# A recurrent-memory attention kernel that plans its own issue order by longest path, with attention for eight heads of both layers at once

## The chip, the cores and the metric

The kernel runs on one core of one Trainium2 chip. Its time is the device time in microseconds (us) of one execution. A time is the median of the runs quoted. The core has a matrix engine (PE, with weight loads shown apart as PEld), a vector engine (DVE), a scalar engine (ACT), a general engine (POOL) and a DMA-issuing engine (SP). The profile also gives the granted clock of the matrix engine: 1.0 is full speed, 0.5 half speed.

## The reference, cut to what matters

```python
def _A_ref(x, mem0, Wq, Wk, Wv, Wo, seg_len):          # 32 heads of 128; x is 2048 x 512
    mem = mem0                                          # 8 rows
    for s in range(n_seg):                              # 64 segments of 32 rows
        h = jnp.concatenate([mem, x[:, s*seg_len:(s+1)*seg_len, :]], axis=1)   # 40 rows
        q, k, v = (einsum('btd,dhe->bhte', h, W) for W in (Wq, Wk, Wv))
        p = _softmax(jnp.where(mask, q @ k.T * scale, -1e9))
        o = einsum('bhte,hed->btd', p @ v, Wo)
        mem = o[:, :M, :]                               # the memory goes into the next segment
        outs.append(o[:, M:, :])
...
x = x + _A_ref(_layernorm(x), A_mem0, A_Wq, A_Wk, A_Wv, A_Wo, A_seg_len)      # layer 1
x = x + _B_ref(_layernorm(x), B_w1, B_w2)                                     # dense 512 -> 1376 -> 512
x = x + _A_ref(_layernorm(x), A_mem0, A_Wq, A_Wk, A_Wv, A_Wo, A_seg_len)      # layer 2, same weights
x = x + _B_ref(_layernorm(x), B_w1, B_w2)
```

Eight rows of each segment's output are the memory of the next, so the 64 segments of a layer are a chain. Both kernels let layer 2 run six segments behind layer 1 and put the two layers' segments side by side: 70 steps, 58 of them with both layers, 12 with one. After every fourth segment of a layer, a group of 128 rows goes through a dense layer and a layernorm.

## The kernel before

The program is written step by step, and the framework's scheduler sets the order on each engine. The recurrent chain has a high priority; what is left fills the gaps.

```python
def layernorm_T(x_g):                 # statistics on DVE and POOL, then a transpose on PE
    ...
    nc.vector.tensor_scalar(out=xn[:], in0=x_g[:], scalar1=mv[:, 0:1], scalar2=rstd[:, 0:1], ...)
    tp = ps_fill.tile([128, NC4, 128], BF, tag="fill")
    for c4 in range(NC4):
        nc.tensor.transpose(tp[:, c4, :], xn[:, c4 * 128:(c4 + 1) * 128], ident[:])
    ...
for k in range(nsteps):
    place_x_values(k); load_group(...); prep_x(k + 1)     # x values: matmuls on 64-column tiles
    with tc.high_priority(offset=PRIO):
        for hf in range(2):                               # 16 heads each
            for (h0, nh) in ((16 * hf, 6), (16 * hf + 6, 6), (16 * hf + 12, 4)):
                qk_batch(HT, h0, nh, a_lo, a_hi)          # 24 (or 16) query, then as many key matmuls: full tiles
            for a in act:
                sps[(a, hf)] = s_matmuls(a, hf)           # mask (full tile) and scores (64-column tiles)
            if hf == 0:
                mem_values(k)                             # 2 x 16 matmuls on 32-column tiles
        for hf in range(2):
            for a in act:                                 # softmax of 16 heads of one layer
                ...                                       # max, subtract: DVE; exp: ACT; sum, reciprocal: DVE
                nc.gpsimd.tensor_tensor(out=P[:, :, b, 0:L], ...)   # product: POOL
        ...                                               # transposes, attention times V (row tiles)
        wo = ...                                          # next memory: 32 matmuls on 32-column tiles
    wx = ...                                              # projection of x rows: 64 matmuls on 32-column tiles
    ...                                                   # residual adds; dense layer when a group is full
```

A "32-column tile" uses a quarter of the array's columns, and four such matmuls for different quarters follow each other; a "row tile" uses part of its rows. In what follows, a change of tile shape is a place in PE's order where a matmul of one class (full tile, 64 columns, 32 columns, row tile) follows one of another. I counted them in the built kernels' order: 2233 in this one.

## Time and profile before

| | before |
|---|---|
| time, median of 3 runs | 2715.88 us (2715.72 to 2721.2) |
| span of the profiled run, granted clock | 2708.6 us, 0.907 |
| PE busy; sum of gaps between its matmuls (idle) | 2278.6 us; 426 us |
| layernorm transposes waiting for DVE | 256.4 us in 63 waits |
| changes of tile shape | 2233 |

From the page of the kernel before: the span, the busy time of each engine, the busy share of PE in 40 slices in tenths, the granted clock in the same slices, and the shares of the chain of work that ended last.

```profile
span 2708.6 us, 89958 instructions
PE 2278.6 (84%) x40852; PEld 1442.6 (53%) x40852; DVE 1271.6 (47%) x2873; ACT 655.5 (24%) x1420; POOL 332.1 (12%) x863
PE   2989878887987978888887987888788797888898
PEclk9999889898898979989898998989888897989999
PE 67%; DVE 18%; POOL 5%; DMA 4%; issue 4%; ACT 1%; SPq 0%; POOLq 0%; ACTq 0%; DVEq 0%
```

PE is the main engine, but most slices stand at 8, and the clock stands at 8 or 7 (below 90%) in 18 of the 40. The waits view names the engine and the line that wait, then whom they wait for, the total us, the times and the longest:

```profile
PE tp L178 <- DVE xn L174: 256.4, 63, 5.1
PE tp L368 <- POOL P_172 L360: 29.2, 64, 1.0
PE tp L368 <- POOL P_166 L360: 21.7, 64, 0.9
```

The layernorm's transposes stand in PE's order about 4 us too early, 63 times, and PE executes in that order. The timeline shows this, and other things (start and length in us, engine and line, output <- inputs, tile, shapes, count, and in brackets the idle time before and what ended it; the length includes the last matmul's modelled end, so rates are read from start to start).

```profile
83.48 0.76 PE L302 MATMUL qp<-HT_156,Wk_sb 128*128 128x40 bf16 x24
84.08 0.75 PE L302 MATMUL qp<-HT_156,Wq_sb 128*128 128x40 bf16 x24
...
88.45 0.77 PE L302 MATMUL qp<-HT_156,Wq_sb 128*128 128x40 bf16 x24
89.19 1.05 PE L282 MATMUL vm<-Wv_sb,HT_156 128*32 128x512 bf16 x16
90.17 0.77 PE L302 MATMUL qp<-HT_156,Wk_sb 128*128 128x40 bf16 x24
...
1308.43 0.61 PE L178 MATMUL tp<-ident,xn 128*128 128x128 bf16 x4 [3.19 <-DVE xn L174]
1313.97 0.61 PE L178 MATMUL tp<-ident,xn 128*128 128x128 bf16 x4 [4.92 <-DVE xn L174]
...
1330.92 3.17 PE L397 MATMUL wo<-Wo_sb,OT 128*32 128x512 bf16 x27
...
1406.10 1.69 PE L397 MATMUL wo<-Wo_sb,OT 128*32 128x512 bf16 x27
```

First: 24 query/key matmuls take 0.60 us where the same shape follows (83.48 to 84.08), and 0.74 us where a 32-column matmul follows (88.45 to 89.19); the change costs 0.14 us there. The 16 memory-value matmuls take 0.98 us before a change, though at 54 ns each they stream for 0.87. Second: the two waits of the layernorm transposes. Third: 27 matmuls of the memory projection take 3.17 us in one step and 1.69 in another. That is the half clock, as the windows view shows around the slow ones (window, its us, PE busy and matmuls, granted clock, DMA share, GB/s):

```profile
1316.00:1318.00 2.00, 2.00 (x12) 0.50 0.00 0
1318.00:1320.00 2.00, 2.00 (x18) 0.83 0.00 0
1320.00:1322.00 2.00, 2.00 (x38) 1.00 0.00 0
...
1326.00:1328.00 2.00, 0.89 (x14) 1.00 0.00 0
1328.00:1330.00 2.00, 2.00 (x39) 0.73 0.00 0
1330.00:1332.00 2.00, 2.00 (x24) 0.50 0.00 0
```

### The profile page before, as it was taken

The page shows a single profiled execution, that of the slowest core. Times are in us where ns is not written, and L with a number is a line of the kernel's source. Part 1 is how long each engine was busy: PE and PEld are TensorE (multiplying, and loading weights), DVE is VectorE, ACT ScalarE, POOL GpSimd, SP SyncE. Part 2 cuts the span into 40 slices and gives each one's busy share as a digit, 9 for nine tenths or more (in the row PEclk, how much of TensorE's full clock was granted, in tenths as well). Part 3 has the DMA queues.
Part 4 walks back from the last instruction along what each step waited for, and adds up shares of the span by engine and source line. Part 5 has one row for each costly group of instructions (what it writes and reads, how often), then busy time and mean ns, then how long its engine had stood idle before and what let it go on. Part 6 is the DMA issues. An engine that isn't in the chain of part 4 may idle for free.

```text
span 2708.6 us, 89958 instructions
## 1 busy us (share of the span) xinstructions
PE 2278.6 (84%) x40852; PEld 1442.6 (53%) x40852; DVE 1271.6 (47%) x2873; ACT 655.5 (24%) x1420; POOL 332.1 (12%) x863
## 2 busy tenths in 40 slices
PE   2989878887987978888887987888788797888898
PEld 1555545555554645555554554555455464555555
DVE  1444445454444445544444454544454444555443
ACT  0222222222222222222222222222222222222222
POOL 2011111011101101101111111111110110111000
PEclk9999889898898979989898998989888897989999
DMA  8000001010001001001001000101100110100000
GB/s 295 16 15 18 21 21 24 13 23 15 21 22 23 18 19 23 16 19 24 15 22 23 16 22 21 24 14 23 23 14 22 23 24 14 23 14 22 18 18 14
DMA packets 39245, 71.52 MB, mean 26 GB/s; under 512 B 13168, under 2 KB 20336, under 8 KB 38864
## 3 DMA queue, kind: packets, MB, share of 16 engines
q1 hardware_dynamic: 33296, 52.34, 8.3%
q8 instruction: 320, 5.24, 0.8%
q10 hardware_dynamic: 3824, 6.78, 0.7%
q0 software_dynamic: 1744, 6.65, 0.7%
q14 instruction: 61, 0.50, 0.1%
HBM read 21.70 MB, written 2.10 MB: 9 GB/s over the span
## 4 chain that ended last, share of the span: by engine, by line
PE 67%; DVE 18%; POOL 5%; DMA 4%; issue 4%; ACT 1%; SPq 0%; POOLq 0%; ACTq 0%; DVEq 0%
PE qp L302 24%; PE vx L257 9%; PE wo L397 7%; PE vm L282 6%; DVE x_g L424 6%; PE wx L417 6%; PE sp L315 3%; PE hp L193 2%; POOL P_172 L360 2%; DVE sm L356 2%; PE sp L311 2%; DVE stats L167 2%; PE tp L178 1%; DVE OT L390 1%; DVE es L352 1%
## 5 line engine op out<-in xcount | busy, mean ns | idle before, releaser
L307 DVE CAST KT<-qp 128x480 bf16<-128x480 f32 (+3 forms) x420 | 237.0, 564 | 416.1 <-PE qp L302 416.0
L302 PEld LDWEIGHTS <-Wq_sb 128*128 128x128 bf16 x8960 | 336.0, 99 | 71.7 <-issue 63.7
L302 PEld LDWEIGHTS <-Wk_sb 128*128 128x128 bf16 x8960 | 344.9, 99 | 25.8 <-issue 23.8
L305 ACT CAST QT<-qp 128x480 bf16<-128x480 f32 (+3 forms) x420 | 203.0, 483 | 400.8 <-PE qp L302 400.7
L417 PE MATMUL wx<-Wo_sb,OT 128*32 128x512 bf16 x4480 | 289.4, 381 | 0.6 <-ACT OT L388 0.6
L424 DVE TENSOR_TENSOR x_g<-x_g,wx 32x512 f32<-32x512 f32 x256 | 175.1, 684 | 186.2 <-PE wx L417 180.8
L397 PE MATMUL wo<-Wo_sb,OT 128*32 128x512 bf16 x2208 | 240.0, 519 | 19.6 <-ACT OT L388 16.0
L178 PE MATMUL tp<-ident,xn 128*128 128x128 bf16 x256 | 40.4, 298 | 256.4 <-DVE xn L174 256.4
L360 POOL TENSOR_TENSOR P_164<-es,sm 128x160 bf16<-128x160 f32 x128 | 55.2, 452 | 1306.1 <-DVE sm L357 1302.1
L257 PE MATMUL vx<-Wv_sb,XS_154 128*64 128x512 bf16 x1120 | 194.9, 406 | 19.2 <-DVE x_g L424 18.1
L302 PE MATMUL qp<-HT_152,Wq_sb 128*128 128x80 bf16 (+1 forms) x4480 | 193.4, 199 | 0.0
L302 PE MATMUL qp<-HT_156,Wq_sb 128*128 128x80 bf16 (+1 forms) x4480 | 192.3, 198 | 0.6 <-DVE HT_156 L409 0.6
L302 PE MATMUL qp<-HT_152,Wk_sb 128*128 128x80 bf16 (+1 forms) x4480 | 186.8, 198 | 3.2 <-DVE KT L307 1.9
L263 DVE CAST vst<-vx 128x512 bf16<-128x512 f32 x140 | 96.5, 689 | 194.9 <-PE vx L257 191.2
L302 PE MATMUL qp<-HT_156,Wk_sb 128*128 128x80 bf16 (+1 forms) x4480 | 186.6, 198 | 1.2
L417 PEld LDWEIGHTS <-OT 128*32 128x32 bf16 x4480 | 110.1, 96 | 128.0 <-issue 28.2
L178 PEld LDWEIGHTS <-xn 128*128 128x128 bf16 x256 | 21.3, 125 | 278.9 <-DVE xn L174 272.5
L257 PE MATMUL vx<-Wv_sb,XS_158 128*64 128x512 bf16 x1120 | 167.3, 448 | 1.7 <-ACT xnT L180 0.7
L350 DVE TENSOR_REDUCE mx<-sp 128x8 f32<-128x320 f32 x256 | 114.8, 487 | 45.4 <-PE sp L315 45.1
L282 PE MATMUL vm<-Wv_sb,HT_152 128*32 128x512 bf16 x1120 | 90.0, 389 | 49.3 <-DVE HT_152 L321 36.4
L354 ACT ACTIVATE es<-es 128x320 f32<-128x320 f32 x256 | 109.7, 468 | 85.4 <-DVE es L352 85.0
L397 PEld LDWEIGHTS <-OT 128*32 128x32 bf16 x2208 | 70.2, 118 | 112.1 <-issue 61.3
(1114 smaller groups left out, 2820.7 us busy)
## 6 DMA issues: line engine op xcount, KB each, us to landing
Vs_162<-vst SPq DMA_DIRECT2D x128, 128.0 KB
Vs_168<-vst SPq DMA_DIRECT2D x128, 128.0 KB
Vs_162<-vms SPq DMA_DIRECT2D x256, 16.0 KB
Vs_168<-vms SPq DMA_DIRECT2D x256, 16.0 KB
Wk_sb<-in_A_Wk_dram ACTq DMA_DIRECT2D x2, 1024.0 KB
Wv_sb<-in_A_Wv_dram POOLq DMA_DIRECT2D x2, 1024.0 KB, 19.1
Wq_sb<-in_A_Wq_dram SPq DMA_DIRECT2D x2, 1024.0 KB
Wo_sb<-in_A_Wo_dram SPq DMA_DIRECT2D x2, 1024.0 KB
```

Source lines behind the costliest of these rows:

```text
L257: nc.tensor.matmul(vx[64 * b:64 * b + 64, :], lhsT=XS[:, c4, :], rhs=Wv_sb[:, c4, n * 512:(n + 1) * 512], start=(c4 == 0), stop=(c4 == NC4 ...
L263: nc.vector.tensor_copy(out=vst[:, p, :], in_=vx[:])
L282: nc.tensor.matmul(vm[32 * q:32 * q + 32, :], lhsT=HT[:, c4, SEG:SEG + 32], rhs=Wv_sb[:, c4, n * 512:(n + 1) * 512], start=(c4 == 0), stop ...
L302: nc.tensor.matmul(qp[:, hi, 0:ncol], lhsT=W_sb[:, c4, h * Dh:(h + 1) * Dh], rhs=HT[:, c4, a_lo * L:a_hi * L], start=(c4 == 0), stop=(c4 = ...
L305: nc.scalar.copy(out=dstT[:, h0:h0 + nh, a_lo * L:a_hi * L], in_=qp[:, 0:nh, 0:ncol])
L307: nc.vector.tensor_copy(out=dstT[:, h0:h0 + nh, a_lo * L:a_hi * L], in_=qp[:, 0:nh, 0:ncol])
L350: nc.vector.tensor_reduce(out=mx[:], in_=sp[:], axis=AX.X, op=ALU.max)
L354: nc.scalar.activation(out=es[:], in_=es[:], func=ACTF.Exp, scale=SCALE)
L360: nc.gpsimd.tensor_tensor(out=P[:, :, b, 0:L], in0=es[:, 4 * b:4 * b + 4, :], in1=sm[:, 4 * b:4 * b + 4].unsqueeze(2).to_broadcast([128, 4 ...
L397: nc.tensor.matmul(wo[32 * q:32 * q + 32, :], lhsT=OT[:, h, SEG:SEG + 32], rhs=Wo_sb[:, h, :], start=(t == 0), stop=(t == H // 4 - 1), til ...
L417: nc.tensor.matmul(wx[32 * q:32 * q + 32, :], lhsT=OT[:, h, XO[a]:XO[a] + SEG], rhs=Wo_sb[:, h, :], start=(t == 0), stop=(t == H // 2 - 1) ...
L424: nc.vector.tensor_tensor(out=rows, in0=rows, in1=wx[r:r + 32, :], op=ALU.add)
```

## The change

Its intent: make attention cheaper per instruction (the softmax of eight heads of both layers at once, query and key banks of four heads emptied by one copy) and remove PE's waits by a plan. The kernel no longer issues as it is written. Every piece of work becomes an operation with an engine, an estimated cost and the data that it reads and writes. A list scheduler then picks, again and again, the engine that can start earliest, and among the operations that can start within 0.05 us of that the one with the longest path of costs and latencies to the end of the program. The kernel emits in that order, and the framework's scheduler is switched off.

```diff
+PE, ACT, DVE, POOL, SP = range(5)
+LAT = (0.26, 0.16, 0.16, 0.20, 1.70)
+LOOK = 0.05
+def t_dve(n, rate=1):
+    return 0.085 + 1.042e-3 * n / rate
...
+    def order(self):
+        for o in reversed(self.ops):
+            o.rank = o.cost + LAT[o.eng] + max((s.rank for s in o.succs), default=0.0)
...
+            lo, e = best                      # earliest start of all, and its engine
+            o = max((c for c in cand[e] if c.start <= lo + LOOK), key=lambda c: (c.rank, -c.seq))
...
-            for hf in range(2):
-                for (h0, nh) in ((16 * hf, 6), (16 * hf + 6, 6), (16 * hf + 12, 4)):
-                    qk_batch(HT, h0, nh, a_lo, a_hi)
+        for p in range(4):                    # eight heads
+            for hg in (2 * p, 2 * p + 1):     # four heads: two operations of 8 matmuls for each of q and k
+                queries_keys(k, hg, a_lo, a_hi)
+            scores(k, p, a_lo, a_hi)          # both layers: one max, subtract, exp, sum, transpose and copy
...
+            for c4 in range(NC4):             # memory values: operations of 4 matmuls
+                def mm(vm=vm, pp=pp, c4=c4): ...
+                plan.op(PE, 0.216, mm, r=[("HTm", i), ("HTx", i, 1), ...], w=[vm])
...
+        for t in range(H // 2):               # x projection: operations of 4 matmuls; x values: of 2
+                plan.op(PE, 0.216, mm, r=[("OT", t // 4), ...], w=[wx])
...
+    with tc.manual_schedule():
+        for o in plan.order():
+            o.fn()
```

The matrix work is the same: 40876 matmuls instead of 40852, the 24 more being mask matmuls. In the new order I counted 4658 changes of tile shape.

## The prediction

> **What bounds the kernel now.** PE is 67% of the chain of waits, DVE 18%; PE is busy 2278.6 of 2708.6 us, not all of it useful. From start-to-start times in the timeline at granted clock 1.0, one matmul costs 35.9 ns (query/key, 80 columns; 25 ns with 40), 54 ns (memory values, both output projections: 32-column tiles), 108 ns (x values: 64-column tiles), 216 ns (second dense product), about 56 ns (first dense product, transposes), 19 to 23 ns (scores, attention). Times the counts: 1780 us. Around each change of tile shape (128, 64, 32 columns, row tiles) about 0.115 us is lost: 16 memory-value matmuls before a query matmul take 0.98 us instead of 0.87, 4 x-value matmuls 0.55 instead of 0.43. The Trainium skill ("TensorEngine Tiling (Array Packing)", Key Properties) says that changing the tiling mode drains the TensorE; the trace agrees. In the issue order I count 2233 changes: 257 us. The mean granted clock of 0.907 means about 250 us lost to half speed: after a 5 us wait, 27 memory-projection matmuls take 3.17 us instead of 1.69. The rest, about 420 us, is idle PE: 256 us in 63 waits of the layernorm transposes for DVE (about 4 us each), 50 at the start, 51 for POOL's softmax product. 1780 + 257 + 250 + 420 = 2707, the span. A full step takes 40.1 us.
>
> **What the change does.** Arithmetic and matmul counts stay (24 more mask matmuls). Query/key evictions become 16 of four heads per step instead of 12; K goes partly to ACT. Estimates from durations: DVE about 80 us less, ACT 130 more; both stay far from full. In the new order, memory values, x values, projections and dense work are cut into pieces of 2 or 4 matmuls, put between query/key groups and into the softmax and layernorm waits.
>
> - Removed: nearly all layernorm waits, most POOL waits, and with them the half clock: idle 420 to about 100 us (55 start, the rest end and steps), clock loss 250 to about 20.
> - Added: the plan's costs know nothing of tile-shape changes. I count 4658, 2425 more: +279 us, all on PE, so on the critical path. A full step has 26.5 us of streaming and about 68 changes (7.8 us): 34.3 us. Steps with one layer active may get slower (about 27 us against 23).
> - Interleaved query and key halves leave about 0.7 us to empty a bank; the pieces between just cover it (eviction 0.43 to 0.49 us plus latencies).
>
> **Prediction.** 1783 + 536 (changes) + 20 (clock) + 100 (idle) = 2440 us, 0.90 of before. Range 2310 to 2580. Faster by over 2%: 0.92; within 2%: 0.05; slower: 0.03.
>
> **What would show it.** PE busy about 95% in all slices, granted clock at least 0.98, the layernorm transposes' wait for DVE under 40 us; in the chain PE at least 85%, DVE under 8%; in the timeline, 4-matmul memory-value pieces between query matmuls at about 0.45 us with both changes (0.22 of it streaming); full steps of 34 to 35 us.
>
> **What would make it wrong.** The cost of a change: 0.08 us would give 2280, 0.15 us 2600; I measured it mostly with long runs on both sides, and short pieces may differ. Waits that the plan doesn't foresee: its DVE and ACT costs are some 15% below the trace's (320 columns on DVE 0.42 planned, 0.49 measured), and the query/key banks or the last-projection chain could leave PE idle 1 to 2 us per step (+70 to 140 us). A clock that drops although PE is nearly always busy.

## The result

| | before | after |
|---|---|---|
| time, median of 4 runs | 2717.56 us (2715.72 to 2721.2) | 2488.48 us (2479.97 to 2492.84) |
| span of the profiled run, granted clock | 2708.6 us, 0.907 | 2478.0 us, 0.979 |
| idle PE | 426 us | 173 us |
| lost to the clock, (1 - clock) x span | 252 us | 52 us |
| of it while PE was busy | 192 us | 48 us |
| changes of tile shape | 2233 | 4658 |

The ratio is 0.9152 (95% interval 0.9122 to 0.9181). The prediction of 2440 us was 48 us too low, and its range holds the result. While PE waits, half clock takes nothing from it; the row "of it while PE was busy" (half of PE's busy time under the trace's records of half clock) leaves that part out.

The lines of the page of the kernel after that answer to those of before:

```profile
span 2478.0 us, 91607 instructions
PE 2300.9 (93%) x40876; PEld 1338.7 (54%) x40876; DVE 1202.9 (49%) x2947; ACT 748.5 (30%) x1818; POOL 343.9 (14%) x910
PE   0899999999999999999999999999999999999998
PEclk9899999998999999999999999999999999999999
```

Its largest waits of PE:

```profile
PE fill_183 L326 <- DVE bf_76 L321: 60.1, 1, 60.1
PE misc_181 L614 <- POOL P_148 L605: 17.4, 6, 2.9
PE fill_184 L326 <- DVE bf_76 L321: 14.9, 10, 3.9
```

The 256 us of layernorm waits are gone but for one at the start (60.1 us) and about 17 us besides. PE stands at 9 in all slices but the first two and the last. Yet PE's busy time has grown, from 2278.6 to 2300.9 us, though the clock is better. The timeline shows why:

```profile
1302.75 0.45 PE L535 MATMUL qk_178<-HT_136,Wq_sb 128*128 128x80 bf16 x8
1303.04 0.45 PE L535 MATMUL qk_177<-HT_136,Wq_sb 128*128 128x80 bf16 x8
1303.42 0.41 PE L469 MATMUL fill_183<-Wv_sb,XS_138 128*64 128x512 bf16 x2
1303.76 0.40 PE L697 MATMUL fill_184<-Wo_sb,OT 128*32 128x512 bf16 x4
1303.98 0.39 PE L503 MATMUL st_182<-Wv_sb,HT_136 128*32 128x512 bf16 x4
1304.30 0.46 PE L535 MATMUL qk_178<-HT_136,Wk_sb 128*128 128x80 bf16 x8
```

Eight query matmuls take 0.29 us before eight of the same shape (1302.75 to 1303.04), and 0.38 before a 64-column matmul. Four 32-column matmuls take 0.22 us before others of that shape (1303.76 to 1303.98), and 0.32 before full tiles. Each change costs some 0.1 us, and nothing in the plan's costs knows of it.

### The profile page after: what moved, and what is told of

Read it like the earlier page. It is cut to its first block, busy times and chain, and to the rows that moved or that the text cites. A ratio compares the mean times of both kernels' runs of the same rounds, so it can differ in the third digit from the quotient of the medians.

```text
span 2478.0 us, 91607 instructions
## 1 busy us (share of the span) xinstructions
PE 2300.9 (93%) x40876; PEld 1338.7 (54%) x40876; DVE 1202.9 (49%) x2947; ACT 748.5 (30%) x1818; POOL 343.9 (14%) x910
## 5 line engine op out<-in xcount | busy, mean ns | idle before, releaser
L535 PEld LDWEIGHTS <-Wq_sb 128*128 128x128 bf16 x8960 | 352.1, 99 | 90.5 <-issue 86.6
L697 PE MATMUL fill_184<-Wo_sb,OT 128*32 128x512 bf16 x2560 | 252.5, 389 | 2.6 <-DVE xg_74 L707 1.7
L659 PE MATMUL st_182<-Wo_sb,OT 128*32 128x512 bf16 x2208 | 225.0, 406 | 3.1 <-ACT OT L442 2.2
L442 ACT CAST QT<-qk_177 128x320 bf16<-128x320 f32 (+1 forms) x279 | 112.5, 403 | 380.1 <-PE qk_177 L535 375.4
L442 ACT CAST QT<-qk_178 128x320 bf16<-128x320 f32 (+1 forms) x281 | 113.5, 404 | 354.3 <-PE qk_178 L535 353.9
L444 DVE CAST KT<-qk_177 128x320 bf16<-128x320 f32 (+1 forms) x218 | 100.3, 460 | 240.9 <-PE qk_177 L535 226.9
L444 DVE CAST KT<-qk_178 128x320 bf16<-128x320 f32 (+1 forms) x202 | 92.7, 459 | 190.3 <-PE qk_178 L535 174.2
L697 PEld LDWEIGHTS <-OT 128*32 128x32 bf16 x4480 | 112.1, 94 | 134.7 <-issue 84.9
L605 POOL TENSOR_TENSOR P_145<-es_162,sm_166 128x160 bf16<-128x160 f32 (+1 forms) x140 | 58.1, 435 | 861.3 <-ACT QT L442 397.8
L697 PE MATMUL fill_183<-Wo_sb,OT 128*32 128x512 bf16 x1920 | 170.2, 385 | 0.0
L469 PE MATMUL fill_183<-Wv_sb,XS_139 128*64 128x512 bf16 x664 | 143.5, 428 | 1.9 <-ACT hT_176 L360 1.9
L535 PE MATMUL qk_177<-HT_136,Wk_sb 128*128 128x80 bf16 (+1 forms) x2256 | 124.7, 199 | 5.0 <-POOL HT_136 L460 4.9
L535 PE MATMUL qk_178<-HT_136,Wk_sb 128*128 128x80 bf16 (+1 forms) x2224 | 122.3, 199 | 4.1 <-POOL HT_136 L460 3.9
L469 PE MATMUL fill_183<-Wv_sb,XS_138 128*64 128x512 bf16 x632 | 125.3, 399 | 0.7
L535 PE MATMUL qk_178<-HT_136,Wq_sb 128*128 128x80 bf16 (+1 forms) x2256 | 125.1, 200 | 0.3 <-DVE KT L444 0.3
L535 PE MATMUL qk_177<-HT_137,Wk_sb 128*128 128x80 bf16 (+1 forms) x2240 | 123.0, 199 | 0.0
L535 PE MATMUL qk_177<-HT_136,Wq_sb 128*128 128x80 bf16 (+1 forms) x2224 | 122.8, 199 | 0.1
L535 PE MATMUL qk_178<-HT_137,Wk_sb 128*128 128x80 bf16 (+1 forms) x2240 | 122.9, 199 | 0.0
L535 PE MATMUL qk_177<-HT_137,Wq_sb 128*128 128x80 bf16 (+1 forms) x2240 | 122.9, 199 | 0.0
L535 PE MATMUL qk_178<-HT_137,Wq_sb 128*128 128x80 bf16 (+1 forms) x2240 | 122.8, 199 | 0.0
L469 PEld LDWEIGHTS <-XS_139 128*64 128x64 bf16 x1120 | 62.9, 112 | 105.4 <-issue 94.5
```

The source lines that it names most:

```text
L442: nc.scalar.copy(out=out_, in_=in_)
L444: nc.vector.tensor_copy(out=out_, in_=in_)
L469: nc.tensor.matmul(vx[64 * b:64 * b + 64, :], lhsT=XS[:, c4, :], rhs=Wv_sb[:, c4, n * 512:(n + 1) * 512], start=(c4 == 0), stop=(c4 == NC4 ...
L535: nc.tensor.matmul(qp[:, hi * 2 * L:hi * 2 * L + n], lhsT=W_sb[:, c4, h * Dh:(h + 1) * Dh], rhs=HT[:, c4, c0:c1], start=(c4 == 0), stop=(c ...
L605: nc.gpsimd.tensor_tensor(out=P[:, a_lo:a_hi, :, b, 0:L], in0=es[:, a_lo:a_hi, b, :, :], in1=s.unsqueeze(3).to_broadcast([128, na, 2, L]), ...
L659: nc.tensor.matmul(wo[32 * q:32 * q + 32, :], lhsT=OT[:, h, SEG:SEG + 32], rhs=Wo_sb[:, h, :], start=(t == 0), stop=(t == H // 4 - 1), til ...
```

## The experiments

My theory had three parts. (1) The gain is idle PE and half clock removed, by the plan. (2) A good part of it is given back by 2425 more changes of tile shape, at about 0.1 us each. (3) The rival explanations are: the grouping of attention by eight heads and the smaller operations do it, whatever the order; or any list scheduling does it, and longest path is no part of it; and for the given-back part, that interleaving costs by waits and not by the changes. All kernels below gave correct results and were timed in 3 rounds. The first four (stay_p16, stay_p4, stay_m16, fifo) ran on one chip (before there: 2714.06 us, median of 7), the other four on another (before: 2708.54 us, median of 7). For the measurement of the kernel after no chip is on record (before there: 2717.56 us).

### A preference for the tile shape that PE has: three doses

The plan's choice gets a bonus for a PE operation whose first matmul has the tile shape that PE's last one had. The bonus is in us of path. Operations, costs and everything else stay. With 16 the plan stays with a shape where it can, with 4 it does so where ranks are close, and with -16 it seeks changes.

```diff
+STAY = 16            # 4 in stay_p4, -16 in stay_m16
...
-            o = max((c for c in cand[e] if c.start <= lo + LOOK), key=lambda c: (c.rank, -c.seq))
+            o = max((c for c in cand[e] if c.start <= lo + LOOK),
+                    key=lambda c: (c.rank + STAY * (e == PE and c.shape[0] == last), -c.seq))
...
+            if e == PE:
+                last = o.shape[1]
...
-                plan.op(PE, 0.216, mm, r=[("XS", i, 0), ("XS", i, 1), ("W", "v", p)],
+                plan.op(PE, 0.216, mm, shape=(64, 64), r=[("XS", i, 0), ("XS", i, 1), ("W", "v", p)],
... (shape of first and last matmul: 32-column pieces (32, 32), scores (128, 64), attention (0, 0), all else (128, 128))
```

Expected of the bonus of 16:

> One key in the planner is changed: among the PE operations that could start now, one of the tile shape that PE has just used gets 16 us added to its rank. Same operations, same costs, same buffers; tile-shape changes in the issue order fall from 4658 to 2388. If a change costs PE about 0.11 us and PE sets the time: 2488 - 2270 x 0.11 = about 2240 us (2200 to 2300). If what is left after the change is waits for other engines and shape changes are hidden or free: about 2490 us, or slower, as the longest path is no longer followed strictly.

Expected of the bonus of 4:

> The same with 4 us added: 3541 changes of tile shape. Shape-change theory: 2488 - 1117 x 0.11 = about 2365 us, up to 40 us more from waits because this plan itself has some more idle PE: 2350 to 2410. Rival (changes are free): about 2490 us or more.

Expected of the bonus of -16:

> The same with 16 us taken away, so that the planner seeks changes: 5957. Shape-change theory: 2488 + 1299 x 0.11 = about 2630 us, perhaps 60 us less since this plan has less idle PE: 2560 to 2640. Rival (changes are free): about 2490 us or less.

Measured:

| kernel | changes | time (range), us | ratio to before | idle PE, us | clock |
|---|---|---|---|---|---|
| stay_p16 | 2388 | 2151.48 (2150.27 to 2152.91) | 0.7934 | 138.1 | 0.997 |
| stay_p4 | 3541 | 2410.52 (2406.27 to 2413.5) | 0.8886 | 205.3 | 0.967 |
| after | 4658 | 2488.48 (2479.97 to 2492.84) | 0.9152 | 173.0 | 0.979 |
| stay_m16 | 5957 | 2535.29 (2531.58 to 2536.88) | 0.9345 | 128.7 | 0.993 |

The page of stay_p16:

```profile
PE 2006.1 (93%) x40798; PEld 1296.1 (60%) x40876; DVE 1195.1 (56%) x2947; ACT 752.1 (35%) x1818; POOL 349.5 (16%) x910
```

Its timeline, with whole runs of one shape where the kernel after has pieces:

```profile
1300.76 1.32 PE L540 MATMUL qk<-HT,Wq_sb 128*128 128x80 bf16 x32
1302.01 0.40 PE L664 MATMUL st<-Wo_sb,OT 128*32 128x512 bf16 x4
1302.34 1.92 PE L474 MATMUL fill<-Wv_sb,XS 128*64 128x512 bf16 x16
```

The page of stay_m16, with the same operations:

```profile
PE 2402.1 (95%) x40795; PEld 1398.9 (55%) x40876; DVE 1206.5 (48%) x2947; ACT 775.9 (31%) x1818; POOL 345.9 (14%) x910
```

And its timeline, where pieces of 4 and 8 matmuls take 0.33 and 0.39 us with a change after each. The last two lines show a change of operation without a change of tile shape:

```profile
1300.88 0.40 PE L508 MATMUL st<-Wv_sb,HT 128*32 128x512 bf16 x4
1301.21 0.46 PE L540 MATMUL qk<-HT,Wq_sb 128*128 128x80 bf16 x8
1301.60 0.40 PE L508 MATMUL st<-Wv_sb,HT 128*32 128x512 bf16 x4
...
1316.01 0.46 PE L540 MATMUL qk<-HT,Wq_sb 128*128 128x80 bf16 x8
1316.31 0.30 PE L564 MATMUL misc<-maskb,ident 128*128 128x320 bf16 x1
```

The time follows the number of changes. The cleanest pair is stay_p16 and stay_m16: same operations, idle PE 138 and 129 us (both traces lack some 80 matmul records, so both are a little too high), clock 0.997 and 0.993, and 3569 more changes take 2535.29 - 2151.48 = 383.8 us, which is 0.1075 us for one. Waits cannot be the reason, as the slower kernel waits less. Nor is it that a piece ends and another operation begins: eight query matmuls take 0.30 us before the mask, which has the same tile shape (1316.01 to 1316.31), and 0.39 us before a 32-column piece. Over the whole trace of stay_m16, the median from a query matmul's start to the next matmul's (full clock, no wait) is 36 ns before another operation of the same shape (88 cases) and 132 ns before another shape (1388 cases). Part 2 of the theory stands, and with it what the change gives back: at 0.1075 us, 2425 more changes cost 261 us; the sum of all runs below gives 226.

The direction was as expected, two of the three times were not: stay_p16 came 49 us below its range and stay_m16 25 us below its; stay_p4 lies at the upper edge of its range. The expectations counted changes alone or nearly so; stay_p16 also has 35 us less idle PE and some 40 us less loss by the clock than the kernel after, and stay_m16 44 and some 34.

"PE busy" can't tell these kernels apart: the fast one is busy for 93% of its span, the slow one for 95%. The Trainium skill ("Perfetto Trace Analysis", Identifying the Most-Contended Engine) warns that matmul busy time is no good measure of how close a kernel is to its limit; here it rises while the kernel gets slower.

The row of the kernel after is from another measurement than the doses, and one dose is not clean: stay_p4 has fewer changes than the kernel after, but 32 us more idle PE and a lower clock (0.967). A new wait of 2.68 us for a layernorm recurs every eight steps in it. Part of what it saves in changes is lost there.

### Program order in place of longest path, without and with the preference

The scheduler and the operations stay; the rank of the longest path is replaced by the place in the program.

```diff
-            o = max((c for c in cand[e] if c.start <= lo + LOOK), key=lambda c: (c.rank, -c.seq))
+            o = max((c for c in cand[e] if c.start <= lo + LOOK), key=lambda c: -c.seq)        # fifo
+            o = max((...), key=lambda c: (STAY * (e == PE and c.shape[0] == last), -c.seq))    # fifo_stay, STAY = 1
```

Expected without the preference:

> Priority by program order in place of the longest path; everything else of the planner stays. 3494 tile-shape changes, 1164 fewer, worth -128 us. If the longest path is what removes PE's idle time, layernorm and softmax waits come back by 150 to 300 us: 2500 to 2650 us. If any greedy planning in time does it, only the fewer changes count: about 2360 us.

Expected with it:

> Program order as priority, and the same tile shape first: 3114 tile-shape changes, 726 more than stay_p16 and 380 fewer than fifo. If only changes count: 2431 - 380 x 0.10 = about 2390 us and 2151 + 73 = about 2225 us cannot both hold; what lies between them is idle PE. I expect 2300 to 2400 us with idle PE near fifo's 230 us, which would show that the longest path is worth 90 us or more of idle PE.

Measured: fifo took 2430.83 us (2425.26 to 2447.01), ratio 0.8972 (0.8935 to 0.9008), with 3494 changes, idle PE 229.5 us and clock 0.978 (the profiled run is the slowest of its four; the others had 0.982 to 0.989). My expectation was a miss: plain program order is not slower than longest path, it is faster than the kernel after by some 50 us (ratios to before 0.8972 and 0.9152, from different measurements). fifo_stay took 2399.43 us (2399.22 to 2405.53), ratio 0.886, with 3114 changes, idle PE 229.9 us and clock 0.979, as expected, at the upper edge of the range. The largest waits of PE in fifo_stay, after that at the start, recur once in nearly every step:

```profile
PE st L664 <- ACT OT L447: 54.3, 68, 0.9
PE misc L639 <- DVE PT L624: 29.8, 67, 0.5
```

So longest path does do something: the idle PE is 173 us with it and 230 without, and with the preference 138 against 230. That is 57 to 92 us. But with nothing against changes, it takes 1164 more of them (4658 against 3494), and at about 0.1 us each these cost more than the waits that it removes. Longest path is worth its trouble only with the preference: 2151 against 2399 us (ratios 0.7934 and 0.886, on two chips), of which 92 us are idle PE, 726 fewer changes give some 70 to 80, and the clock (loss of 6 against 50 us) some 44; about 40 us of the difference are in none of these terms.

### The half clock by itself

In the kernel before, useless matmuls are put in front of each layernorm's transposes, into the bank that these will overwrite. This takes none of the real work away, and the real work waits as before; it only keeps PE busy in the gap.

```diff
-        tp = ps_fill.tile([128, NC4, 128], BF, tag="fill")
+        tpf = ps_fill.tile([128, 512], F32, tag="fill")
+        for _ in range(12):
+            nc.tensor.matmul(tpf[:], lhsT=ident[:], rhs=Wq_sb[:, 0, 0:512], start=True, stop=True)
+        tp = tpf[:].bitcast(BF)
```

> The kernel before, with twelve useless 128x512 matmuls before each layernorm's transposes, into the bank that the transposes overwrite: 64 x 12 x 0.216 = 166 us of extra work at full clock. The issue order puts them exactly into the layernorm waits and moves nothing else. If the rests of PE cost about 250 us through the clock: granted clock from 0.907 to 0.95 or more, and the kernel gets faster although it does more, 2500 to 2640 us. If the idle time alone cost: no faster than before, 2715 to 2880 us.

Measured: 2659.24 us (2653.8 to 2662.75), ratio 0.9811 (0.9788 to 0.9834), clock 0.951. The transposes' wait fell from 256.4 to 80.6 us:

```profile
PE tpf L182 <- DVE xn L175: 80.6, 59, 2.3
```

This kernel does 768 more matmuls, which take 166 us even at full clock, and it is faster by 1.9%: clear of zero, but at the line of 2% the verdict is "unclear". It came out above the expected range (2500 to 2640 us), and the traces show why the clock was worth less than I thought. By the mean clock, the loss went from 252 to 130 us. But of 506 us at half clock in the kernel before, PE was idle for 122; counted while PE was busy, the loss went from 192 to 130 us. With 178 us less idle PE, 166 us more work and 122 more changes (2355, about 12 us), these 62 us make some 60 us; the spans differ by 49. So the half clock is a cost of its own. What remains of it is in its windows, at the same place of a step as in the kernel before:

```profile
1298.00:1300.00 2.00, 0.89 (x15) 1.00 0.00 0
1300.00:1302.00 2.00, 2.00 (x38) 0.68 0.00 0
1302.00:1304.00 2.00, 2.00 (x28) 0.50 0.00 0
```

In this stretch PE's single gaps were 0.52 us (before the memory projection, for an eviction by ACT) and 0.60 us (before x values, for DVE), and no more than the 0.89 of 2 us were busy. The clock fell to half all the same. The Trainium skill ("TensorE: Matmul & The Clock Gate", Part 1) has the clock halved after an idle window of about 3.4 us. The waits of 3.19 and 4.92 us before 1314 agree roughly: the clock fell at 1308.4, at the end of the shorter one, when PE had been busy for 0.07 of the last 3.41 us. The same page (A second HAM failure mode) says that PE can also idle in small gaps often enough for the clock to swing between half and full; this trace agrees, with two gaps of 0.5 and 0.6 us in two us. It does not always happen: at 1402 to 1404 in the kernel before, PE was also busy for 0.89 of 2 us, and the clock stayed at 1.00. In that kernel the clock changes on a grid of 3.41 us; PE was busy for 0.67 of the grid's interval before the fall at 1328.9, and for 0.68 of that before 1404.0, where none came. So the busy share of that interval does not decide it, and what does is open.

### The new operations under the framework's scheduler

The operations of the kernel after are emitted in program order, with the priorities of the kernel before, and the framework's scheduler orders them. Buffers are taken in turn. One ring of four buffers replaces the three rings for transposed groups.

```diff
-    with tc.manual_schedule():
-        for o in plan.order():
-            o.fn()
+    for o in plan.order():                  # now the program's order
+        if o.high:                          # the recurrent chain, as before
+            with tc.high_priority(offset=10_000_000):
+                o.fn()
+        else:
+            o.fn()
```

> The changed kernel's operations (8 heads of both layers per softmax, four-head evictions), but emitted in program order and ordered by the framework's scheduler with the same priorities as the kernel before; its own planner is out. One shared ring of four for the transposed activations, as before. Tile-shape changes in the issue order: 7848, single matmuls between single matmuls. If the planned order is what gained: slower than before, 2750 to 3050 us. If the new grouping of the attention gained: about 2490 us.

Measured: 3396.87 us (3376.76 to 3422.35), ratio 1.254 (1.2469 to 1.2611), with 7848 changes, idle PE 353.4 us and clock 0.93. Slower, as the theory said, but by more than expected. The timeline shows single memory-value matmuls between single query and key matmuls, and further on four together:

```profile
1310.36 0.39 PE L476 MATMUL st<-Wv_sb,HT 128*32 128x512 bf16 x1
1310.68 0.21 PE L508 MATMUL qk<-HT,Wq_sb 128*128 128x80 bf16 x1
...
1311.35 0.40 PE L476 MATMUL st<-Wv_sb,HT 128*32 128x512 bf16 x4
1311.68 0.21 PE L508 MATMUL qk<-HT,Wq_sb 128*128 128x80 bf16 x1
```

So the regrouping alone brought no gain that shows, and the rival that "the grouping does it, whatever the order" is refuted for this scheduler. What the grouping is worth in an order of its own with as few changes as the kernel before is not separated: this run has 5615 more changes than before. Why it is so slow can be read from its trace. The one 32-column matmul at 1310.36 takes 0.32 us up to the next, and the four at 1311.35 take 0.33: a lone one costs as much as four, so a group of four that is broken pays twice. The framework's scheduler moves single matmuls, and here 1209 of 1649 runs of 32-column matmuls are no whole groups of four (nor are 188 of 380 runs of 64-column ones whole pairs). Counted at 0.216 us for each group begun, the empty quarters and halves cost about 199 us, an estimate. The kernel before has the same fault: 398 of 584 runs, about 60 us. The planned kernels have none, as their operations of 4 and 2 matmuls stay whole. So by this count part of the plan's gain is that it keeps these groups together, which I had not thought of; no run isolates it.

### The start, and the fastest version

At the start of the kernel after, PE waits 60 us. The timeline of DVE shows what for:

```profile
58.93 0.43 DVE L405 CAST xg_73<-bf_76 128x512 f32<-128x512 bf16 x1 [23.25 <-DMA bf_76<-in_A_x_dram]
...
59.47 0.55 DVE L321 TENSOR_SCALAR bf_76<-xg_72,ln_170 128x512 bf16<-128x512 f32 x1
```

The plan believes that the second group of rows is loaded in about 2 us, and puts its conversion ahead of the first group's normalisation in DVE's order. But its load stands behind the weights in its queue. The last experiment adds to stay_p16 that this data is there only after 48 us:

```diff
             x, xb = p_x.buf(), p_b.buf()
+            plan.available(xb, 48.0)
```

> stay_p16 with the loads of x after the first marked as not available to the plan before 48 us, so that the first layernorm no longer waits in DVE's queue behind a copy of x group 1, whose load stands behind the weights in the queue. PE's first wait of 60 us should become about 36 us (the memory's load lands there); by then not all weights are there: 2125 to 2145 us against 2151.

Measured: 2125.16 us (2124.81 to 2126.25), ratio 0.7843 (0.7825 to 0.7861), 26 us less than stay_p16 (the two ran on different chips; their ratios to before there are 0.7843 and 0.7934), with idle PE 106.9 us. The first wait of PE in its timeline:

```profile
36.90 0.61 PE L331 MATMUL fill<-ident,bf 128*128 128x128 bf16 x4 [36.90 <-DVE bf L326]
```

It is the fastest version, 22% below the kernel before and some 14% below the kernel after (0.7843 against 0.9152 of before). In the kernel before, PE's first matmul ran at 36.42 us, so 24 us of the start were the plan's doing, through one wrong belief.

### All runs in one sum

For each kernel, the span less idle PE, less the loss by the clock while PE is busy, less the broken groups, less 1783 us of streaming (an estimate: counts times the rates read at full clock; 1949 us in warm), divided by the number of changes:

| kernel | span, us | idle | clock loss, PE busy | broken groups | changes | rest for one change, us |
|---|---|---|---|---|---|---|
| before | 2708.6 | 426 | 192 | 60 | 2233 | 0.111 |
| warm | 2659.4 | 248 | 130 | 63 | 2355 | 0.115 |
| after | 2478.0 | 173 | 48 | 0 | 4658 | 0.102 |
| stay_p16 | 2148.6 | 138 | 6 | 0 | 2388 | 0.093 |
| stay_p4 | 2404.5 | 205 | 71 | 0 | 3541 | 0.098 |
| stay_m16 | 2535.2 | 129 | 15 | 0 | 5957 | 0.102 |
| fifo | 2444.8 | 230 | 52 | 0 | 3494 | 0.109 |
| fifo_stay | 2397.3 | 230 | 47 | 0 | 3114 | 0.108 |
| stay_x | 2123.3 | 107 | 4 | 0 | 2392 | 0.096 |
| own_sched | 3375.1 | 353 | 184 | 199 | 7848 | 0.109 |

All ten kernels, from 2123 to 3375 us, are told by the same four terms, with 0.093 to 0.115 us for a change. The rests are good to some hundredths of a us only: the streaming is an estimate, and the score matmuls, taken at 19 to 23 ns, follow each other at 13 to 14 ns in these traces (means at full clock), so that it may be some tens of us too high.

## Why the prediction was right, and where its terms were off

- **The time, 2440 us, range 2310 to 2580.** Measured 2488.48. The way to it held: 1783 us of streaming, fewer waits, less half clock, more changes.
- **"Idle 420 to about 100 us."** It went from 426 to 173. This is the term that was mis-sized most (+73 us). The start took 60 us and not 55, and about 45 us are stalls that recur every eight steps: 2.9 and 2.3 us for POOL's softmax product, 1.0 for a layernorm, 1.0 for POOL's copy of x rows into HT, the input of the queries and keys. That the wait for POOL comes from the plan's order on DVE was only argued.
- **"Clock loss 250 to about 20."** 48 us on busy PE (52 by the mean clock); the clock was 0.979 and not "at least 0.98". The 250 us of the kernel before were too many: 192 of them fell on busy PE (the rest on waits that were counted already).
- **"4658, 2425 more: +279 us."** The count was exact; a change cost 0.102 us by the sum and 0.1075 between the two clean doses, not 0.115. By the sum this made the prediction too high by 62 us (536 to 474), so that the three errors, +73, +28 and -62, leave 39 us, and that they cancel so far is luck; the median is another 10 us longer than the profiled span. It was right that the changes lie on the critical path. The Trainium skill ("TensorEngine Tiling (Array Packing)", Key Properties) says that changing the tiling mode drains the TensorE; the doses agree in that each change costs, but no run shows that a drain is what takes the time.
- **"1780 + 257 + 250 + 420 = 2707, the span."** That this came out to the microsecond was luck as well: the clock's loss was 58 us too high, and some 60 us of broken groups were missing.
- **"After a 5 us wait, 27 memory-projection matmuls take 3.17 us."** The half clock was right, the cause wrong: the windows show the clock back at 1.00 from 1320 to 1328, and down again after two gaps of 0.51 and 0.60 us. The 5 us wait slowed other matmuls, up to 1318.
- **"PE busy about 95% in all slices."** 93%, all slices at 9 except the first two and the last. **"Layernorm transposes' wait under 40 us."** About 17, if the first wait of 60 us, which is the start, is left out; with it 77. **"PE at least 85% of the chain, DVE under 8%."** Not tested: in the kernel after, this view follows the chain for only a small part of the span.
- **"Pieces at about 0.45 us with both changes."** A four-matmul piece showed 0.33 instead of 0.22 before a change, and the query matmuls ahead of it 0.38 instead of 0.29: 0.42 us for piece and both changes.
- **"Full steps of 34 to 35 us."** 35.4 on average between two copies of the new memory (about 40 before), but uneven, from 30 to 50 us. **"Steps with one layer may get slower (27 us against 23)."** Not in sum: the first five such intervals take 24.4 to 29.5 us against 23.0 to 25.3 and one of 42.0, and the first and last five together 275 us against 282.
- **"Removed by the plan."** I took for granted that longest path is what removes the waits. It removes 57 to 92 us of idle PE, and the rest the same planner and operations remove in program order: fifo has 230 us where the kernel before has 426. By itself, longest path costs more in changes than it saves.
- **DVE "about 80 us less, ACT 130 more."** 69 less (1271.6 to 1202.9) and 93 more (655.5 to 748.5). No run tests whether it mattered; PE was busy for 93% of the span.

In sum, the change took about 253 us of idle PE, 144 us of half clock and 60 us of broken groups away and gave some 226 (by the sum) to 261 us (by the doses) back in changes of tile shape. With half of the changes avoided and the first loads timed rightly, the same plan reaches 2125 us.

## What to carry to other kernels

A plan finds only the costs that it is told of: when a list scheduler cuts matmul runs into pieces, give it the cost of a change of tile shape, or a preference for the present shape, before refining its priorities. Keep the matmuls that fill one group of column tiles together. Count the changes in the issue order and set them beside idle PE and the granted clock; PE's busy share tells none of them. And see what the plan believes of the first loads, as one wrong arrival time cost some 24 us here.

## What the Trainium skill lacked or had wrong

- "TensorEngine Tiling (Array Packing)", Key Properties, says that a change of tiling mode drains the TensorE, but has no cost for it: here 0.1075 us for one, from two orders of the same operations with 2388 and 5957 changes, and 0.093 to 0.115 us in ten kernels. Nor has the page what a broken group of column tiles costs: one 32-column matmul took 0.32 us before a change, and four took 0.33.
- "Perfetto Trace Analysis", Optimization Strategy, advises to interleave regimes that are limited by different engines. It lacks the warning that interleaving small pieces of matmuls of different tile shapes costs PE time: 2535.29 against 2151.48 us for the same work.
- "TensorE: Matmul & The Clock Gate", A second HAM failure mode, has no size for the small gaps that halve the clock. Here two gaps of 0.5 and 0.6 us in a stretch of 2 us with PE busy for 0.89 were enough in two kernels (granted clock 1.00, then 0.50), and a like stretch elsewhere in the same kernel was not.
